# A tuned state-space and gated-MLP kernel: the first table load ahead of two weight loads, tile 1's gate steps split around later transposes, a gated load queue, two warm-up matmuls fewer

## The chip, the cores and the metric

The kernel runs on one core of one Trainium2 chip. Its time is the device time of one execution in microseconds (us); the figure for a kernel is the median of several runs. A core has five engines that run side by side: TensorE (PE, matmuls; PEld is its weight loads), VectorE (DVE), ScalarE (ACT), GpSimd (POOL) and SyncE (SP, here a queue that only issues transfers). Each takes its instructions in the order in which they were written for it, and waits on semaphores for the others.

## The reference

The input x is 2048 tokens of 448 features, in bf16. It is normalised, and two branches use the result: a diagonal complex state-space recurrence (A) and a gated MLP (B).

```python
xn = _layernorm(x, axis=-1)
s = _A_ref(xn, A_Lambda_re, ..., A_Dskip)
g = _silu(_B_ref(xn, B_w_gate, B_w_up, B_w_down))
return x + s * g

# A: per state p, over 2048 steps
Lam_bar = exp(dt * Lam)
Bu = einsum("bld,pd->blp", x, ((Lam_bar - 1) / Lam)[:, None] * Bmat)
h = Lam_bar * h + Bu[:, t]
y = 2 * einsum("blp,dp->bld", hseq, Cmat).real + x * Dskip
# B: 448 -> 1792 -> 448
h = sigmoid(x @ w_gate) * (x @ w_up)
return h @ w_down
```

## The kernel before

The tokens go in four chunks of 512, a chunk being four tiles of 128 tokens. For each chunk TensorE computes 14 gate and up steps of 128 columns (`gu_mm`, L767 and L768: two matmuls at a time, on the two halves of the array's rows), the input products of the recurrence (L841 to L858), the down projection (L983) and the output of the recurrence (L1012). ScalarE evacuates the gates (L801), VectorE the up products (L804) and does the recurrence as a scan (L922).

Only the head differs between the kernels: the time until the first chunk's normalised x stands transposed in SBUF. Tiles 0 to 3 of chunk 0 go through it one by one:

- `load_x` brings tile t; tiles 0 and 2 are issued on SP's queue, 1 and 3 on ScalarE's. `load_w0` brings the first two 128-column blocks of the gate weights (m = 0 and 1) in four parts: A and B for each half of the partitions; the rest of the gate weights (`load_w("SP", "g", ...)`), x for chunk 1, and the up weights follow on SP's queue.
- VectorE takes mean and variance (`bn` L448, `aggr` L454), ScalarE the square root (`root` L482, which needs the square-root table, L412), VectorE the reciprocal (`recip` L479) and the normalised tile (`norm` L515). GpSimd appends a copy of the first 64 columns (L524).
- TensorE transposes the tile against the identity (`pe_transpose` L552, and L554 for the piece that needs GpSimd's copy) into two banks: pieces 4 to 6 make half "b", pieces 0 to 3 half "a". Each half is copied to SBUF by ScalarE (L562) or VectorE (L564), as `split` says.
- `last_tile` (L784 and L785) runs the gate steps m = 0 and 1 for one tile alone, its half "b" or "a". For tiles 0, 1 and 3 this helper is used, for tile 2 `gu_mm` (L767 and L768, 128 columns wide). Step m = 2 is the first over all 512 tokens.
- `columns` (L596, L598) turns three small parameter rows into columns, in the bank `acc[0]` that tile 0's half b has left; ScalarE copies them out (L603), and GpSimd computes the rotation angles from them (`turns`, L614 on). `silu_table` loads ScalarE's second table (L626).
- Before all that, TensorE runs warm-up matmuls on zeros (`warm_mm`, L442).

The order of the work on each engine is made at build time. `Plan.add` takes each operation with an estimated cost, `Plan.solve` computes due times from the order of TensorE's operations and then lists the others by them. TensorE's order is the order of the calls. While `pl.seq` is set (the head), VectorE's and ScalarE's orders are the order of the calls too; operations with `chain=True` keep their order on their engine. `slot` counts the transfers: the ninth waits for the first, and so on.

Of the kernel before, what the change touches and what calls it, by code (L numbers as in the profile page):

```python
# [14 lines left out]
ACT = mybir.ActivationFunctionType  # L15
# [11 lines left out]
TPC = L // P  # L27
# [219 lines left out]
def kernel(  # L247
# [118 lines left out]
    def load_w(eng, k, half, b, r=(), rate=105e3, land=0.0):  # L366
        m0, m1 = BLK[k][b]
        ps = slice(half * H, half * H + H)
        c0 = half * 896
        load(eng, [("w", k, half, m) for m in range(m0, m1)], H * 7 * (m1 - m0) * P * 2,  # L370
             wgt[k][ps, :, m0 * P:m1 * P],
             wsrc[k][:, c0 + m0 * P:c0 + m1 * P].rearrange("(s p) f -> p s f", p=H), cost=0.65, r=r, rate=rate, land=land)

    def load_w0(eng, half, part, land=0.0):
        ps = slice(half * H, half * H + H)
        s0, c0 = (1 - half if part == "A" else half), half * 896
        n = 4 - s0
        load(eng, [("w", "g", half, m, part) for m in range(2)], H * n * 2 * P * 2, wgt["g"][ps, s0:7:2, 0:2 * P],
             wsrc["g"][:, c0:c0 + 2 * P].rearrange("(s p) f -> p s f", p=H)[:, s0:7:2, :], cost=0.5, rate=400e3, land=land)
# [22 lines left out]
    def load_p(eng, k, r=()):  # L402
# [2 lines left out]
    load_x(1, 1, "ACT")  # L405
    load_x(2, 1, "SP", rate=180e3)
    load_x(3, 1, "ACT", rate=180e3)
    load_w0("SP", 0, "A", land=6.5)
    load_w0("ACT", 1, "A", land=6.7)
    load_w0("SP", 0, "B", land=7.2)  # L410
    load_w0("ACT", 1, "B", land=7.5)
    add("ACT", 0.05, lambda: A.preload_act_table_set("sqrt_and_others"), w=["sqrttab"], lat=1.3, chain=True)  # L412
    load_w("SP", "g", 0, 1, rate=400e3, land=8.8)
    load_w("SP", "g", 1, 1, rate=400e3, land=9.8)
    load_w("SP", "g", 0, 2, rate=400e3, land=11.2)
    load_w("SP", "g", 1, 2, rate=400e3, land=12.6)
    load_x(4, 2, land=14.0)
    load_p("POOL", 0)
    load_p("POOL", 1)
    load_p("POOL", 2)  # L420
    add("POOL", 0.15, lambda: G.memset(ident[:], 0.0), w=["ident"], chain=True)
    add("POOL", 0.4, lambda: G.affine_select(out=ident[:], in_=ident[:], compare_op=ALU.not_equal, fill=1.0, base=0,
                                             pattern=[[-1, P]], channel_multiplier=1), r=["ident"], w=["ident"], chain=True)
    add("POOL", 0.1, lambda: G.memset(halfc[:], 0.5), w=["consts"])
    add("POOL", 0.1, lambda: G.memset(negc[:], -1.0), r=["consts"], w=["consts"])
    add("POOL", 0.1, lambda: G.memset(expc[:], math.e), w=["expc"])
# [18 lines left out]

    def bn(t):
        b = t % 3
        add("DVE", 0.6, lambda: V.bn_stats(out=bst[b][:], in_=x_all[:, t, :]),  # L448
            r=[("x", t)] + ([("xnT", 0, 3, "a")] if 3 < t < 8 else []), w=[("bst", b)])

    def aggr(t):
        b = t % 3
        o = (mvf if t < TPC else mv)[:, t, :]
        add("DVE", 0.16, lambda: V.bn_aggr(out=o, in_=bst[b][:]), r=[("bst", b)], w=[("mv", t)])  # L454

    def stats(t):
        bn(t)
# [18 lines left out]

    def recip(t0, n):
        ks = lambda k: [(k, t) for t in range(t0, t0 + n)]
        add("DVE", 0.13, lambda: V.reciprocal(out=rsd[:, t0:t0 + n, :], in_=sdb[:, t0:t0 + n, :]), r=ks("sd"), w=ks("rs"))  # L479

    def root(t):
        add("ACT", 0.3, lambda: A.activation(sdb[:, t, :], mvf[:, t, 1:2], ACT.Sqrt, bias=epsc[:]),  # L482
            r=[("mv", t), "sqrttab", "epsc"], w=[("sd", t)])

    def chain(t0, n):
        ts = range(t0, t0 + n)
# [25 lines left out]
    def norm(t):  # L512
        b, o = xkey(t), xbuf(t)
        if t < TPC:
            add("DVE", 0.42, lambda: V.tensor_scalar(out=o[:, 0:448], in0=x_all[:, t, :],  # L515
                                                     scalar1=mvf[:, t, 0:1], scalar2=rsd[:, t, :],
                                                     op0=ALU.subtract, op1=ALU.mult),
                r=[("x", t), ("mv", t), ("rs", t)], w=[("xn", b)])
        else:
            add("ACT", 0.65, lambda: A.activation(o[:, 0:448], x_all[:, t, :], ACT.Identity,  # L520
                                                 bias=nmr[:, t, :], scale=rsd[:, t, :]),
                r=[("x", t), ("rs", t), ("nm", t)], w=[("xn", b)])
        n = H if t < TPC else D
        add("POOL", 0.25 if n == H else 0.6, lambda: G.tensor_copy(out=o[:, D:D + n], in_=o[:, 0:n]),  # L524
            r=[("xn", b)], w=[("xnw", b)])
# [16 lines left out]
    def pe_transpose(t, parts, between=None):  # L542
        b, js, o = xkey(t), slice(t * P, t * P + P), xbuf(t)
        tp = {}
        for lo, hi, key, bank, eng in parts:
            for s in range(lo, hi):
                tp[s] = flat(bank.bitcast(BF16)[:, 0:(hi - lo) * P], hi - lo, P)[:, s - lo, :]

        def f():
            for s in (4, 5, 6, 0, 1, 2):  # L550
                c0 = s * P if s < 4 else H + (s - 4) * P
                T.transpose(tp[s], o[:, c0:c0 + P], ident[:, :])  # L552
        add("PE", 0.34, f, r=[("xn", b), "ident"], w=[p[2] for p in parts])
        add("PE", 0.06, lambda: T.transpose(tp[3], o[:, 384:512], ident[:, :]), r=[("xnw", b)], w=[parts[-1][2]])  # L554
        for i, (lo, hi, key, bank, eng) in enumerate(parts):
            if i and between:
                between()
            n = (hi - lo) * P
            w = [("xnT", 0, t, h) for h in (("a" if lo == 0 else "b") if len(parts) == 2 else "ab")]
            src = flat(bank.bitcast(BF16)[:, 0:n], hi - lo, P)  # L560
            if eng == "ACT":
                add("ACT", 0.05 + n / 1120.0, lambda src=src, lo=lo, hi=hi: A.copy(out=xnT[0][:, lo:hi, js], in_=src), r=[key], w=w)  # L562
            else:
                add("DVE", 0.07 + n / 1600.0, lambda src=src, lo=lo, hi=hi: V.tensor_copy(out=xnT[0][:, lo:hi, js], in_=src), r=[key], w=w)  # L564
# [60 lines left out]
    def silu_table():  # L625
        add("ACT", 1.3, lambda: A.preload_act_table_set("silu_and_others"), r=[("sd", t) for t in range(4)] + [("xnT", 0, 2, "a")], w=["silutab"])  # L626

    def tables():
        turn = C("turn")
        for pt in range(4):  # L630
            vk, nk = ("v", pt), ("nu", pt)
            v, nu = v_t[:, pt, :], nu_t[:, pt, :]
            add("ACT", 0.61, lambda v=v, pt=pt: A.activation(v, iota[:, 0:NTAB], ACT.Copy, scale=turn[:, pt:pt + 1]),
                r=[("wv", 0), "turn", "silutab"], w=[vk])
            add("DVE", 0.4, lambda v=v, nu=nu: V.tensor_single_scalar(out=nu, in_=v, scalar=MAGIC, op=ALU.add),
                r=[vk], w=[nk])
            add("DVE", 0.6, lambda v=v, nu=nu: V.scalar_tensor_tensor(out=nu, in0=nu, scalar=-MAGIC, in1=v,
                                                                      op0=ALU.add, op1=ALU.subtract),
                r=[vk, nk], w=[nk])
            add("ACT", 0.5, lambda v=v, nu=nu: A.activation(v, nu, ACT.Abs), r=[nk, "silutab"], w=[vk])  # L640
            so, co = (spm[:, pt, 0, :], cosT[:, pt, :]) if pt < 3 else (cs3[:, 1, :], cs3[:, 0, :])
            add("ACT", 0.537, lambda so=so, nu=nu: A.activation(so, nu[:, 0:L], ACT.Sin, scale=-S),
                r=[nk, "silutab"], w=[("sin", pt)])
            add("ACT", 0.624, lambda co=co, v=v: A.activation(co, v[:, 0:L], ACT.Sin, scale=-S, bias=pio2[:]),
                r=[vk, "silutab", "pio2"], w=[("cos", pt)])
            if pt < 3:
                add("DVE", 0.2, lambda pt=pt: V.tensor_single_scalar(out=spm[:, pt, 1, :], in_=spm[:, pt, 0, :],
                                                                     scalar=-1.0, op=ALU.mult),
                    r=[("sin", pt)], w=[("nsin", pt)])
# [390 lines left out]


    warm_mm(9)
    warm_mm(2, 128)
    pl.seq = True
    slots0 = [next_gu() for _ in range(3)]
    u2 = slots0[2]
# [16 lines left out]
    bn(3)  # L1063
    root(2)
    aggr(3)
    split(1, uk, ub, ("ACT", "ACT"), lambda: root(3))
    recip(2, 1)
    norm(2)
    last_tile(0, "g", steps01, 0, "b")
    pv_copy = columns(acc[0][:], ("acc", 0))  # L1070
    pv_copy()
    last_tile(0, "g", steps01, 0, "a")
    recip(3, 1)
    norm(3)
    last_tile(0, "g", steps01, 1)
    add("NONE", 0.0, lambda: None, r=["pv0", ("xnw", 3)], w=["pv"], lat=0.0)
    turns()
    split(2, ak, ab, ("ACT", "DVE"))
    split(3, uk, ub, ("DVE", "DVE"))
    gate(uk, ("gu", u2))  # L1080
    silu_table()
    pl.seq = False
    for m in range(2):
        gu_mm(0, "g", m, slots0[m], 2, 3, m == 0)
    last_tile(0, "g", steps01, 3)
# [112 lines left out]
```

## Time and profile before

| | |
|---|---|
| median of 3 runs | 185.27 us (185.1 to 185.68) |
| the profiled execution | 184.37 us |
| its span (first to last instruction) | 182.6 us |
| PE busy | 177.6 us, 97% |
| DVE / ACT / POOL busy | 165.8 / 96.9 / 39.7 us |
| chain that ended last | PE 93%, DVE 3% |
| gate step m = 2 starts | 11.40 us |
| up step m = 0 starts | 18.95 us |

Times in the views are microseconds from the start of the span. In a timeline a row gives the start, the time taken, the engine, the line of the kernel, the operation, what it writes and reads, and how many instructions were merged; in brackets stands how long the engine had been idle and what ended that. A "q" behind an engine's name (SPq, ACTq) is its queue issuing transfers. The chain of waits goes back from the last instruction and gives at each step what released it. Matmuls are pipelined: a record lasts longer than the distance to the next one, so rates are read from starts.

### The profile page before, as it was taken

To read this page: it belongs to the slowest core of one execution; us is meant where nothing else is said; L and a number is where in the kernel's file an instruction comes from. 1 tells how busy PE (TensorE), PEld (TensorE's weight loads), DVE (VectorE), ACT (ScalarE), POOL (GpSimd) and SP (SyncE) were. 2 spreads that over 40 slices of the span, in tenths; PEclk is the share of its full clock that TensorE was granted. 3 is DMA by queue.
4 is the path that set the end of the run, shared out by engine and by line. 5 is a ranking of instruction groups with operands and counts; after the bars stand their busy time and mean duration, and the time that the engine had idled before them with its cause. 6 is when DMAs were issued, how large, how long until landed. Compare 5 with 4: busy or idle time off the path is not lost.

```text
span 182.6 us, 3617 instructions
## 1 busy us (share of the span) xinstructions
PE 177.6 (97%) x1412; PEld 89.9 (49%) x1412; DVE 165.8 (91%) x295; ACT 96.9 (53%) x158; POOL 39.7 (22%) x95
## 2 busy tenths in 40 slices
PE   7999999999999999999999999999999999999992
PEld 2775555564554444445554444444555444455551
DVE  3759799899989899999999999999999999999763
ACT  3699997959698796364145543348110533411100
POOL 6383458000049956400004100000000000000000
PEclk9999999999999999999999999999999999999999
DMA  5999999998000290000004900002000000002120
GB/s 150 239 222 219 204 163 165 342 153 242 6 0 0 51 154 0 4 0 0 0 2 82 148 0 0 4 0 70 9 0 0 25 27 29 0 5 71 56 77 25
DMA packets 29938, 13.43 MB, mean 74 GB/s; under 512 B 19424, under 2 KB 29920, under 8 KB 29920
## 3 DMA queue, kind: packets, MB, share of 16 engines
q1 hardware_dynamic: 29056, 12.74, 33.9%
q10 hardware_dynamic: 768, 0.46, 0.9%
q8 instruction: 11, 0.18, 0.4%
q14 instruction: 7, 0.06, 0.1%
q0 software_dynamic: 96, 0.00, 0.0%
HBM read 6.77 MB, written 1.84 MB: 47 GB/s over the span
## 4 chain that ended last, share of the span: by engine, by line
PE 93%; DVE 3%; POOL 1%; issue 1%; ACT 1%; DVEq 0%; POOLq 0%
PE gu L767 43%; PE gu L983 15%; PE acc L1012 11%; PE acc L983 9%; PE gu L855 9%; PE acc L858 2%; PE gu L841 2%; PE gu L768 2%; POOL hF L357 1%; PE acc L767 1%; DVE bst L448 1%; PE gu L784 1%; DVE g_t L515 0%; ACT sdb L482 0%; DVE o_t L1028 0%
## 5 line engine op out<-in xcount | busy, mean ns | idle before, releaser
L767 PE MATMUL gu<-xnT,wU 64*128 64x512 bf16 x196 | 45.8, 376 | 0.0
L768 PE MATMUL gu<-xnT,wU 64*128 64x512 bf16 x196 | 45.8, 376 | 0.0
L767 PE MATMUL gu<-xnT,wG 64*128 64x512 bf16 (+2 forms) x203 | 42.3, 350 | 0.1
L768 PE MATMUL gu<-xnT,wG 64*128 64x512 bf16 (+2 forms) x203 | 42.3, 350 | 0.0
L801 ACT ACTIVATE sig<-gu 128x1024 f32<-128x1024 f32 x21 | 21.3, 1020 | 23.7 <-PE gu L768 19.1
L983 PEld LDWEIGHTS <-hF 128*128 128x128 bf16 x224 | 21.9, 98 | 20.6
L767 PEld LDWEIGHTS <-wU 64*128 64x128 bf16 x196 | 18.4, 94 | 22.1
L767 PEld LDWEIGHTS <-wG 64*128 64x128 bf16 x210 | 19.2, 94 | 19.4
L983 PE MATMUL gu<-wd,hF 128*128 128x448 bf16 x140 | 28.0, 352 | 0.0
L804 DVE SCALAR_TENSOR_TENSOR hF<-sig,gu 128x1024 bf16<-128x1024 f32 x21 | 25.4, 1210 | 1.2 <-ACT sig L801 1.0
L922 DVE TENSOR_TENSOR_SCAN wv<-c_r,st,z 128x512 bf16<-128x512 f32 x18 | 22.9, 1277 | 0.0
L1012 PE MATMUL acc<-cT,hT 128*128 128x448 bf16 (+1 forms) x112 | 22.6, 346 | 0.0
L989 ACT ACTIVATE g_t<-gu 128x448 bf16<-128x448 f32 x10 | 5.4, 542 | 27.7 <-PE gu L983 16.8
L768 PEld LDWEIGHTS <-wG 64*128 64x128 bf16 x210 | 19.2, 94 | 0.1
L768 PEld LDWEIGHTS <-wU 64*128 64x128 bf16 x196 | 18.4, 94 | 0.0
L983 PE MATMUL acc<-wd,hF 128*128 128x448 bf16 x84 | 16.9, 352 | 0.0
L855 PE MATMUL gu<-xnT,bT 128*128 128x512 bf16 x72 | 16.7, 379 | 0.0
L1012 PEld LDWEIGHTS <-hT 128*128 128x128 bf16 x119 | 11.5, 98 | 10.1 <-issue 0.4
L869 ACT CAST bus<-gu 128x1024 bf16<-128x1024 f32 x12 | 12.0, 1011 | 6.0 <-PE gu L841 5.5
L524 POOL COPY xn<-xn 128x448 bf16<-128x448 bf16 x12 | 8.2, 698 | 26.2 <-ACT xn L520 26.0
L1024 DVE TENSOR_TENSOR o_t<-acc,xd 128x448 bf16<-128x448 f32 (+1 forms) x16 | 9.6, 601 | 2.7 <-PE acc L1012 2.6
L875 ACT CAST bus<-acc 64x256 bf16<-64x256 f32 (+1 forms) x24 | 8.7, 369 | 5.6 <-PE acc L858 5.3
(149 smaller groups left out, 260.0 us busy)
## 6 DMA issues: line engine op xcount, KB each, us to landing
out_dram<-o_t SPq DMA_DIRECT2D x15, 112.0 KB, 1.7
wd<-in_B_w_down_dram SPq DMA_DIRECT2D x2, 784.0 KB, 6.9
wU<-in_B_w_up_dram SPq DMA_DIRECT2D x2, 448.0 KB, 11.6
x_all<-in_A_x_dram SPq DMA_DIRECT2D x2, 448.0 KB, 4.6
wG<-in_B_w_gate_dram SPq DMA_DIRECT2D x2, 336.0 KB, 6.3
wU<-in_B_w_up_dram SPq DMA_DIRECT2D x2, 336.0 KB, 9.0
wG<-in_B_w_gate_dram SPq DMA_DIRECT2D x2, 224.0 KB, 4.7
x_all<-in_A_x_dram SPq DMA_DIRECT2D x2, 224.0 KB, 8.9
```

The source lines that it names most:

```text
L524: add("POOL", 0.25 if n == H else 0.6, lambda: G.tensor_copy(out=o[:, D:D + n], in_=o[:, 0:n]), r=[("xn", b)], w=[("xnw", b)])
L767: T.matmul(bank[0][:, ts], lhsT=w_[0:H, s, ms], rhs=x[0:H, SL[s], ts], start=(s == 0), stop=(s == 6))
L768: T.matmul(bank[1][:, ts], lhsT=w_[H:P, (s + 1) % 7, ms], rhs=x[H:P, SL[s], ts], start=(s == 0), stop=(s == 6))
L801: add("ACT", act(1024), lambda: A.activation(th, gu[a][:], ACT.Tanh, scale=0.5), r=[("gu", a)], w=[tk])
L804: add("DVE", dve1(1024), lambda: V.scalar_tensor_tensor(out=ho, in0=th, scalar=1.0, in1=gu[a][:], op0=ALU.add, op1=ALU.mult), r=[("gu", a) ...
L855: T.matmul(gu[slots[pt]][:, i, :], lhsT=bT[:, kt, i, pt * P:pt * P + P], rhs=x[:, kt, :], start=(first and kt == 0), stop=(not first and k ...
L869: add("ACT", act(1024), lambda: A.copy(out=bus[u][:], in_=gu[slots[pt]][:]), r=key(pt), w=[("bus", u)])
L875: add("ACT", 0.36, lambda ns=ns, d=d, q=q, l=l, i=i: A.copy(out=bus[u][d, l, ns], in_=acc[a3[i]][q, 0:256]), r=[("acc", a3[i])] + ([("bus" ...
L922: dve(1.194, lambda k=k: V.tensor_tensor_scan(out=wv[:, k, :], data0=rb, data1=z[:, k, :], initial=(st[pt][:, k, :] if c else 0.0), op0=AL ...
L983: T.matmul(d, lhsT=hF[c % 2][:, m, h, js], rhs=wd[:, ft, :], start=(ft == 0), stop=(ft == FT - 1))
L1012: T.matmul(y, lhsT=hT[c % 2][:, hm, js], rhs=cT[:, cm, c0:c1], start=(i == 0 and not on_pe), stop=(i == 6))
L1024: add("DVE", dve1(n), lambda od=od, y=y, c0=c0, c1=c1: V.tensor_tensor(out=od, in0=y, in1=xq[:, c0:c1], op=ALU.add), r=[key, ("xd", q)], w ...
```

## The change

The square-root table load is written before ScalarE's two weight loads, not behind them. The remaining gate weights are written behind the identity and a small GpSimd memset into the region that the first of these loads fills, so that this load waits for the memset. Inside tile 1's evacuation, tile 0's half b steps, the columns and their copy come before the third root; of tile 1's gate steps, half b stays and half a goes behind the transposes of tiles 2 and 3. The first `Copy` of the tables (L633) is issued in the head's fixed order. The two 128-column warm-up matmuls are gone. Several estimates of costs and landing times for the planner are altered (only some are shown).

```diff
     load_x(3, 1, "ACT", rate=180e3)
-    load_w0("SP", 0, "A", land=6.5)
-    load_w0("ACT", 1, "A", land=6.7)
-    load_w0("SP", 0, "B", land=7.2)
-    load_w0("ACT", 1, "B", land=7.5)
     add("ACT", 0.05, lambda: A.preload_act_table_set("sqrt_and_others"), w=["sqrttab"], lat=1.3, chain=True)
-    load_w("SP", "g", 0, 1, rate=400e3, land=8.8)
-    load_w("SP", "g", 1, 1, rate=400e3, land=9.8)
-    load_w("SP", "g", 0, 2, rate=400e3, land=11.2)
-    load_w("SP", "g", 1, 2, rate=400e3, land=12.6)
-    load_x(4, 2, land=14.0)
+    load_w0("SP", 0, "A", land=5.7)
+    load_w0("ACT", 1, "A", land=5.9)
+    load_w0("SP", 0, "B", land=6.9)
+    load_w0("ACT", 1, "B", land=6.9)
     load_p("POOL", 0)
     load_p("POOL", 1)
     load_p("POOL", 2)
     add("POOL", 0.15, lambda: G.memset(ident[:], 0.0), w=["ident"], chain=True)
     add("POOL", 0.4, lambda: G.affine_select(out=ident[:], ...
+    add("POOL", 0.1, lambda: G.memset(wgt["g"][0:1, 0, 256:258], 0.0), w=[("w", "g", 0, m) for m in (2, 3)], chain=True)
+    load_w("SP", "g", 0, 1, rate=400e3, land=8.8)
+    load_w("SP", "g", 1, 1, rate=400e3, land=9.8)
+    load_w("SP", "g", 0, 2, rate=400e3, land=11.2)
+    load_w("SP", "g", 1, 2, rate=400e3, land=12.6)
+    load_x(4, 2, land=14.0)
...
-        add("PE", 0.34, f, r=[("xn", b), "ident"], w=[p[2] for p in parts])
+        add("PE", 0.64 if t < 2 else 0.34, f, r=[("xn", b), "ident"], w=[p[2] for p in parts])
...
+    def scale(pt):
+        turn, v = C("turn"), v_t[:, pt, :]
+        add("ACT", 0.61, lambda: A.activation(v, iota[:, 0:NTAB], ACT.Copy, scale=turn[:, pt:pt + 1]),
+            r=[("wv", 0), "turn", "silutab"], w=[("v", pt)])
+
     def tables():
...
-            add("ACT", 0.61, lambda v=v, pt=pt: A.activation(v, iota[:, 0:NTAB], ACT.Copy, scale=turn[:, pt:pt + 1]),
-                r=[("wv", 0), "turn", "silutab"], w=[vk])
+            if pt:
+                scale(pt)
...
     warm_mm(9)
-    warm_mm(2, 128)
...
     root(2)
     aggr(3)
-    split(1, uk, ub, ("ACT", "ACT"), lambda: root(3))
+
+    def pv_root():
+        last_tile(0, "g", steps01, 0, "b")
+        columns(acc[0][:], ("acc", 0))()
+        root(3)
+    split(1, uk, ub, ("ACT", "ACT"), pv_root)
     recip(2, 1)
     norm(2)
-    last_tile(0, "g", steps01, 0, "b")
-    pv_copy = columns(acc[0][:], ("acc", 0))
-    pv_copy()
     last_tile(0, "g", steps01, 0, "a")
+    last_tile(0, "g", steps01, 1, "b")
     recip(3, 1)
     norm(3)
-    last_tile(0, "g", steps01, 1)
     add("NONE", 0.0, lambda: None, r=["pv0", ("xnw", 3)], w=["pv"], lat=0.0)
     turns()
     split(2, ak, ab, ("ACT", "DVE"))
     split(3, uk, ub, ("DVE", "DVE"))
     gate(uk, ("gu", u2))
     silu_table()
+    scale(0)
     pl.seq = False
+    last_tile(0, "g", steps01, 1, "a")
     for m in range(2):
         gu_mm(0, "g", m, slots0[m], 2, 3, m == 0)
     last_tile(0, "g", steps01, 3)
```

More of the change, by code (lines that the diff above doesn't have):

```diff
@@ L447, in bn @@
         b = t % 3
-        add("DVE", 0.6, lambda: V.bn_stats(out=bst[b][:], in_=x_all[:, t, :]),
+        add("DVE", 0.56 if t < TPC else 0.6, lambda: V.bn_stats(out=bst[b][:], in_=x_all[:, t, :]),
             r=[("x", t)] + ([("xnT", 0, 3, "a")] if 3 < t < 8 else []), w=[("bst", b)])
@@ L453, in aggr @@
         o = (mvf if t < TPC else mv)[:, t, :]
-        add("DVE", 0.16, lambda: V.bn_aggr(out=o, in_=bst[b][:]), r=[("bst", b)], w=[("mv", t)])
+        add("DVE", 0.1 if t < TPC else 0.16, lambda: V.bn_aggr(out=o, in_=bst[b][:]), r=[("bst", b)], w=[("mv", t)])
     def stats(t):
@@ L478, in recip @@
         ks = lambda k: [(k, t) for t in range(t0, t0 + n)]
-        add("DVE", 0.13, lambda: V.reciprocal(out=rsd[:, t0:t0 + n, :], in_=sdb[:, t0:t0 + n, :]), r=ks("sd"), w=ks("rs"))
+        add("DVE", 0.08, lambda: V.reciprocal(out=rsd[:, t0:t0 + n, :], in_=sdb[:, t0:t0 + n, :]), r=ks("sd"), w=ks("rs"))
     def root(t):
-        add("ACT", 0.3, lambda: A.activation(sdb[:, t, :], mvf[:, t, 1:2], ACT.Sqrt, bias=epsc[:]),
-            r=[("mv", t), "sqrttab", "epsc"], w=[("sd", t)])
+        add("ACT", 0.2, lambda: A.activation(sdb[:, t, :], mvf[:, t, 1:2], ACT.Sqrt, bias=epsc[:]),
+            r=[("mv", t), "sqrttab", "epsc"], w=[("sd", t)], lat=0.16)
     def chain(t0, n):
@@ L514, in norm @@
         if t < TPC:
-            add("DVE", 0.42, lambda: V.tensor_scalar(out=o[:, 0:448], in0=x_all[:, t, :],
+            add("DVE", 0.33, lambda: V.tensor_scalar(out=o[:, 0:448], in0=x_all[:, t, :],
                                                      scalar1=mvf[:, t, 0:1], scalar2=rsd[:, t, :],
@@ L552, in f @@
                 T.transpose(tp[s], o[:, c0:c0 + P], ident[:, :])
-        add("PE", 0.34, f, r=[("xn", b), "ident"], w=[p[2] for p in parts])
-        add("PE", 0.06, lambda: T.transpose(tp[3], o[:, 384:512], ident[:, :]), r=[("xnw", b)], w=[parts[-1][2]])
+        add("PE", 0.64 if t < 2 else 0.34, f, r=[("xn", b), "ident"], w=[p[2] for p in parts])
+        add("PE", 0.1 if t < 2 else 0.06, lambda: T.transpose(tp[3], o[:, 384:512], ident[:, :]), r=[("xnw", b)], w=[parts[-1][2]])
         for i, (lo, hi, key, bank, eng) in enumerate(parts):
@@ L626, in silu_table @@
         add("ACT", 1.3, lambda: A.preload_act_table_set("silu_and_others"), r=[("sd", t) for t in range(4)] + [("xnT", 0, 2, "a")], w=["silutab"])
+    def scale(pt):
+        turn, v = C("turn"), v_t[:, pt, :]
+        add("ACT", 0.61, lambda: A.activation(v, iota[:, 0:NTAB], ACT.Copy, scale=turn[:, pt:pt + 1]),
+            r=[("wv", 0), "turn", "silutab"], w=[("v", pt)])
     def tables():
-        turn = C("turn")
         for pt in range(4):
```

## The prediction

> **What bounds the kernel now.** I read the page's busy shares and its chain first, then a table of stretches, then the chain of waits in the first ten microseconds, then each engine's timeline there.
>
> From the page, the busy shares:
>
> ```profile
> PE 177.6 (97%) x1412; PEld 89.9 (49%) x1412; DVE 165.8 (91%) x295; ACT 96.9 (53%) x158; POOL 39.7 (22%) x95
> ```
>
> From the table of stretches (stretch, its length, busy time of PE, PEld, DVE, ACT and POOL with instruction counts, then granted clock, DMA share, GB/s):
>
> ```profile
> 7.93:8.20 0.27, 0.16 (x6) 0.04 (x1) 0.27 (x1) 0.27 (x2) 0.20 (x1) 1.00 0.97 252
> ...
> 9.72:9.84 0.12, 0.00 (x1) 0.01 (x2) 0.08 (x2) 0.12 (x1) 0.12 (x1) 1.00 1.07 265
> ...
> 11.40:178.00 166.60, 166.60 (x1256) 82.56 (x1250) 158.10 (x270) 90.26 (x146) 33.15 (x68) 1.00 0.33 66
> ```
>
> From 11.40 us, where the gate step m=2 starts, to 178.00 TensorE has no idle time. So the end is that start plus a constant, and whatever the head gains or loses is found again at the end, as long as no wait appears later. TensorE is idle in the head: before 8.20 its only records are the tails of pipelined matmuls, and before 9.84 it does nothing. The chain of waits says who ends these gaps:
>
> ```profile
> 4.35 0.29 ACT sdb L482
> 4.64 0.02 issue
> 4.66 0.16 DVE rsd L479
> 4.83 0.08 DVE mvf L454
> 4.91 0.35 DVE g_t L515
> ...
> 5.87 0.55 DVE bst L448
> ...
> 6.62 0.52 DVE bst L448
> ...
> 7.38 0.30 ACT sdb L482
> 7.68 0.48 ACT xnT L562
> ...
> 8.82 0.44 PE acc L552 x6
> ...
> 9.36 0.44 DVE xnT L564
> ```
>
> Three things last: the first root (L482) starts late and holds VectorE's chain of statistics; ScalarE's second copy of tile 1 (7.58 to 8.15) holds tile 1's second half of gate steps at 8.20, and behind these in TensorE's order stand the transposes of tiles 2 and 3, whose input was ready at 7.83 (tile 2, L515); VectorE's copy of tile 2 (9.36 to 9.78) holds the steps of 9.84. Why the root is late, from ScalarE's timeline:
>
> ```profile
> 1.66 1.34 ACTq L357 DMA_DIRECT2D wG<-in_B_w_gate_dram  x2
> 3.04 1.28 ACT L412 ACT_TABLE_LOAD   x1 [3.04 <-issue]
> 4.33 0.30 ACT L482 ACTIVATE sdb<-mvf,epsc 128x1 bf16<-128x1 f32 x1
> ```
>
> The root starts where the table load ends (3.04 + 1.28 = 4.32). Its variance was ready at 3.96 (L454, 3.78 + 0.18). The chain names a GpSimd memset as its releaser, but that ends at 4.34, after the root's start, and the memset of epsc that the root reads ends at 3.67.
>
> **Part 1: the table load before the two weight loads on ScalarE's queue.** It would start at 1.66 and end at 2.94, under the wait for x. The root is then bound by its variance: 3.96 + 0.04 (the gap from L454 to the second root: 4.74 + 0.16 to 4.94) = 4.00 instead of 4.33. VectorE gets less of it, since it is in bn_stats of tile 1 until 3.88 + 0.59 = 4.47; that tile's aggregate then starts at 4.51 instead of 4.74. All later VectorE steps move by that 0.23: norms at 4.63, 5.24, 7.20 and 7.70, tile 0's transposes at 5.08, tile 1's at 5.69, tile 0's first gate steps at 6.19 (6.42 before). They read the weight halves A, landed by 1.66 + 4.1 = 5.76. No row shows whether a transfer is issued while a table load runs. Bounds: the issues go out at 1.66 as now (cost nothing), or at 2.94 (1.28 later). I take the first: the profile books issues to ACTq and table loads to ACT. In the second case the root is again behind the two issues (2.94 + 1.34 = 4.28), the 0.23 is lost and the first gate steps wait for a later half A.
>
> [...]
>
> **Part 2: tile 1's gate steps split.** Order on TensorE now: tile 0 (halves b, columns, a), tile 1 (b, a), transposes 2, transposes 3, steps of tile 2. After: tile 1's b, transposes 2 and 3, tile 1's a, steps of tile 2. Nothing is added; the two waits get cover:
> - Tile 1's a follows transposes 3, at about 8.7. Its copy now ends at 8.15; it moves 0.23 earlier with the roots and 0.18 later behind the copy of the columns (L603, 0.18), so it ends near 8.1. The 0.27 of idle before 8.20 goes.
> - Transposes of tile 2 start at about 7.8 (their norm ends at 7.60), not 8.75. VectorE's copy of tile 2 then runs 8.41 to 8.83, under tile 1's a (8 slots of 56 ns, 0.45, until 9.14). The gap of 9.49 to 9.84 falls from 0.35 between starts to the 0.15 seen at the same change of work at 6.27 to 6.42: 0.20 goes.
> - Tile 3's copies (0.69 for both) end near 9.5, before its steps at 9.9.
>
> **Part 3: columns' copy ahead of the third root.** The root of tile 3 needs its aggregate at 7.12 and the copy ends at 7.24, so that root is some 0.1 later than it could be; tile 3's norm (7.70) is needed only by 8.2. Free. GpSimd's chain starts after tile 3's pad copy in both.
>
> **Part 4: SP's loads of blocks 1 and 2 behind a GpSimd memset.** The memset stands after the identity, at about 3.57, and lasts 0.10 like its neighbours; epsc moves 0.04, with 0.3 to spare. The first load now issues at 3.31 and would at 3.72: +0.41, with everything queued behind it on SP (the rest of wG, x 4 to 7, wU, dbc, the transposes of B). Landings now are 7.8 and 8.8 (issue 3.31 + 4.5, 4.02 + 4.8), against the need at 10.75; the second half of wU's first block lands at 7.34 + 10.1 = 17.44, against a need at 18.95 - 0.65 = 18.3. Even the whole 0.41 leaves 0.45. It need not arrive, as the transfers' share is full from 2 us on and x and the first weights are still landing until 6.9. For the same reason I book no gain for the first weight halves. Half B, issued at 2.42, lands at 6.92 (+ 4.5), and this now matters: tile 0's second half would be ready to run at 6.90. Bounds: 0.3 later (a share of the ring lost to something else) to 0.2 earlier; I take 6.92, start 6.95.
>
> **Part 5: two 128-column warm-up matmuls gone** (4.99 to 5.3). TensorE waits for the norm there anyway, so the time itself is free; what they do for TensorE's pace is the first rival. The first scaling of the position table (L633) joins the written order where it already ran, behind the second table load (10.93), and the changed cost figures alter only the planner's order, for which the last rival stands.
>
> **The sum.** From tile 0's second half to step m=2: now 7.13 to 11.40 = 4.27, less 0.27 and 0.20 of idle = 3.80. After: 6.95 + 3.80 = 10.75, that is 0.65 earlier. The profiled execution took 184.37 (span 182.6 and 1.77 around it): 183.72. The median of the runs is 0.90 above it; taking the same 0.65 off 185.27 gives **184.62**. Later covers hold: VectorE waits 1.22 us for TensorE at 172.32, and the last state write for chunk 3 ends at 167.6, against its first use at 170.8.
>
> **The rivals.**
> *Slower: TensorE's slow pace lasts longer.* The page prints a granted clock of 1.00 throughout, but the warm-up matmuls start 0.427 apart (loads of weights at 1.58, 2.01, 2.44) where the same 512 columns later take 0.215 (11.40, 11.61, 11.83). The pace rises while tile 0 is transposed: its six take 0.59, tile 1's 0.51.
>
> ```profile
> 5.31 0.59 PE L552 MATMUL acc<-ident,g_t 128*128 128x128 bf16 x6
> ...
> 5.92 0.51 PE L552 MATMUL gu<-ident,g_t 128*128 128x128 bf16 x6
> ```
>
> After the change the warm-up ends near 5.0 and its end is what keeps TensorE busy until then. At half pace each slot of 128 columns costs 0.055 more. Tiles 1 to 3's transposes and the steps between are 41 slots: 2.26 at worst, 186.9. The point of decision is 12 slots (0.65 / 0.055) for no gain, 22 for a loss that can be measured; I price it at 30, 1.65 - 0.65 = +1.0, **186.3**. Against it: TensorE's gap before the transposes stays at 0.1 (now 5.10 + 0.11 to 5.31; after, 4.57 + 0.43 to 5.08), so it is no less busy than now.
>
> [...]
>
> *Partial.* The same slow pace over tiles 0 and 1 only (up to the copies' own pace): 7 slots are 0.39 off the gain, or half B lands 0.3 later: gain 0.25 to 0.5, **184.9**.
>
> *The table load blocks ScalarE's queue* (the change doesn't do what it says): the 0.23 is gone and half A lands up to 0.5 later; part 2 remains: gain about 0.2, **185.05**.
>
> *A later wait.* Earlier due times reorder VectorE or ScalarE behind TensorE. Nothing in the trace shows one; from -0.1 to a copy's length, +1.2: **185.6**.
>
> **How the numbers follow.** Forecast 0.54 (own range 184.4 to 184.8), partial 0.20, blocked queue 0.06, slow pace 0.14, later wait 0.06. 0.3% is 0.56 us, about what a measurement of this kernel can tell from no change. Faster by more: nearly all of the forecast, 0.52. Slower by more: the slow pace and part of the later wait, 0.18. Within: 0.30. The range runs from 184.2 (half B early, and the runs' own scatter of 0.2) to 186.0, leaving out the upper part of the slow pace.
>
> **What would show it.** Right: table load at 1.7, first root at 4.0, tile 2's transposes at 7.8, no TensorE gap after 7.0, step m=2 at 10.7 to 10.8. Wrong: weight issues on ACTq after 2.9; transposes of tile 1 taking 0.7; m=2 later than 11.1; any TensorE gap after it.

## The result, and the profile after

The changed kernel took **184.24 us** (median of 12 runs, 184.01 to 185.0) against 185.05 for the kernel before in the runs beside it (12 runs, 184.45 to 185.68): ratio 0.996, 95% interval 0.9943 to 0.9976, that is 0.4 to 1.05 us less. Two later series gave 0.9958 (0.9941 to 0.9975) and 0.9956 (0.9936 to 0.9975). The forecast was 184.62, a gain of 0.65; measured were 0.81, 0.68 and 0.78. The comparison moved from 185.27 to 185.05 with more runs, which is 0.22 of the 0.38 by which the time lies below the forecast.

The profiled execution of the changed kernel, though, took 184.25 us with a span of 182.4, only 0.12 below the profiled one before, and not 0.65. From its page, the busy shares:

```profile
PE 177.7 (97%) x1410; PEld 88.8 (49%) x1410; DVE 166.3 (91%) x295; ACT 97.0 (53%) x158; POOL 38.1 (21%) x96
```

They say nothing of the change but the two matmuls fewer. The table of stretches, from a little before tile 0's first gate steps to step m=2, and from there to 178.00 (columns as in the prediction):

```profile
6.50:11.26 4.76, 4.76 (x134) 4.22 (x134) 2.81 (x9) 3.44 (x9) 2.53 (x9) 1.00 1.04 229
11.26:178.00 166.74, 166.74 (x1256) 81.47 (x1251) 158.60 (x270) 90.84 (x146) 31.92 (x70) 1.00 0.34 67
```

Both gaps of before (0.27 and 0.20) are gone and no new one has appeared; yet m=2 starts at 11.26, not 10.75. ScalarE's timeline (rows as in the prediction) shows the first half of the change at work:

```profile
1.66 1.28 ACT L408 ACT_TABLE_LOAD   x1 [1.66 <-PEq L1190]
1.69 1.60 ACTq L357 DMA_DIRECT2D wG<-in_B_w_gate_dram  x2
4.15 0.30 ACT L483 ACTIVATE sdb<-mvf,epsc 128x1 bf16<-128x1 f32 x1 [1.21 <-DVE mvf L455]
```

The table load starts at 1.66, and the two weight issues run beside it from 1.69: the load does not hold the queue. The root waits for its variance now (L455), at 4.15. So 0.18 of the hoped 0.33 came. The rest of the lateness is in TensorE's timeline, the transposes of tiles 0 and 1:

```profile
5.13 0.82 PE L553 MATMUL acc<-ident,g_t 128*128 128x128 bf16 x6
5.75 0.31 PE L555 MATMUL acc<-ident,g_t 128*128 128x128 bf16 x1
5.85 0.85 PE L553 MATMUL gu<-ident,g_t 128*128 128x128 bf16 x6
6.49 0.31 PE L555 MATMUL gu<-ident,g_t 128*128 128x128 bf16 x1
```

Six transposes take 0.82 and 0.85, against 0.59 and 0.51 before. From the first of six to the seventh it is 5.75 - 5.13 = 0.62, or 0.103 each; at full pace, for tile 2 of the same profile, it is 8.70 - 8.35 = 0.35, or 0.058 each. In the table of stretches TensorE is "busy" all this time and its granted clock is printed as 1.00:

```profile
4.00:6.00 2.00, 2.00 (x12) 1.02 (x11) 1.89 (x8) 0.93 (x3) 0.81 (x5) 1.00 0.86 234
```

So neither column shows the half pace; starts do. The chain of waits agrees: from the warm-up matmuls on it never leaves TensorE.

```profile
3.49 1.71 PE gu L443 x4
5.20 0.75 PE acc L553 x6
5.95 0.11 PE acc L555
6.06 0.64 PE gu L553 x6
6.70 0.11 PE gu L555
```

The same kernel profiled again (run `e5_after`: 183.64 us, span 181.9) has full pace from tile 0 on:

```profile
4.99 0.51 PE L553 MATMUL acc<-ident,g_t 128*128 128x128 bf16 x6 [0.34 <-DVE g_t L516]
5.34 0.22 PE L555 MATMUL acc<-ident,g_t 128*128 128x128 bf16 x1
5.66 0.51 PE L553 MATMUL gu<-ident,g_t 128*128 128x128 bf16 x6
```

There the root is at 4.01, tile 2's transposes at 7.76 and m=2 at 10.67: the forecast's timeline (4.00, 7.8, 10.75) and its time for the profiled execution (183.72).

### The profile page after: what moved, and what is told of

Same layout as the page of the kernel before. It is cut to its first block, busy times and chain, and to the rows that moved or that the text cites. A ratio compares the mean times of both kernels' runs of the same rounds, so it can differ in the third digit from the quotient of the medians.

```text
span 182.4 us, 3618 instructions
## 1 busy us (share of the span) xinstructions
PE 177.7 (97%) x1410; PEld 88.8 (49%) x1410; DVE 166.3 (91%) x295; ACT 97.0 (53%) x158; POOL 38.1 (21%) x96
## 4 chain that ended last, share of the span: by engine, by line
PE 97%; DVE 1%; issue 0%; DVEq 0%
PE gu L772 44%; PE gu L988 15%; PE acc L1017 11%; PE acc L988 9%; PE gu L860 9%; PE gu L443 2%; PE acc L863 2%; PE gu L846 2%; PE gu L789 1%; PE acc L772 1%; PE gu L773 1%; PE acc L553 1%; PE gu L553 1%; DVE o_t L1033 0%; PE acc L849 0%; DVE o_t L1029 0%
## 5 line engine op out<-in xcount | busy, mean ns | idle before, releaser
L449 DVE BATCH_NORM_STATS2 bst<-x_all 128x6 f32<-128x448 bf16 x12 | 7.0, 611 | 6.7 <-DMA x_all<-in_A_x_dram 6.7
```

The lines of the kernel that those rows point to most:

```text
L449: add("DVE", 0.56 if t < TPC else 0.6, lambda: V.bn_stats(out=bst[b][:], in_=x_all[:, t, :]), r=[("x", t)] + ([("xnT", 0, 3, "a")] if 3 < ...
```

## The experiments

Each row is read from a run's TensorE timeline and from its series. "Half a" is the start of tile 0's second half of gate steps, "x0" the start of tile 0's bn_stats, "six" the time of the six transposes of tiles 0 and 1. The comparison is with the kernel before in the same series: its own median moved between 184.41 and 185.05 from one series to the next, so medians of different series can be compared only loosely.

| run | x0 | root | six | half a | m=2 | difference | median; before beside it | ratio, 95% |
|---|---|---|---|---|---|---|---|---|
| before | 3.12 | 4.33 | 0.59, 0.51 | 7.14 | 11.40 | 4.26 | | |
| after | 3.21 | 4.15 | 0.82, 0.85 | 7.46 | 11.26 | 3.80 | 184.24; 185.05 | 0.996 (0.9943 to 0.9976) |
| e1_nogate | 3.12 | 4.06 | 0.82, 0.60 | 7.47 | 12.19 | 4.72 | 185.14; 184.41 | 1.0037 (1.0012 to 1.0063) |
| e2_warm11 | 3.29 | 4.24 | 0.51, 0.51 | 7.10 | 10.89 | 3.79 | 184.22; 184.41 | 0.9995 (0.9972 to 1.0017) |
| e3_table | 3.25 | 4.20 | 0.51, 0.51 | 7.06 | 11.76 | 4.70 | 185.07; 184.41 | 1.0027 (1.0016 to 1.0039) |
| e4_split | 3.26 | 4.34 | 0.51, 0.51 | 7.14 | 10.94 | 3.80 | 183.95; 184.41 | 0.9969 (0.9958 to 0.998) |
| e5_after | 3.07 | 4.01 | 0.51, 0.51 | 6.87 | 10.67 | 3.80 | 184.06; 184.74 | 0.9958 (0.9941 to 0.9975) |
| e6_split_gate | 3.27 | 4.33 | 0.82, 0.64 | 7.38 | 11.18 | 3.80 | 184.11; 184.74 | 0.9966 (0.9952 to 0.998) |
| e7_split_table_1b | 3.30 | 4.24 | 0.51, 0.51 | 7.10 | 10.90 | 3.80 | 183.94; 184.74 | 0.9955 (0.9938 to 0.9972) |
| e8_warm4 | 3.22 | 4.33 | 0.82, 0.85 | 7.98 | 12.07 | 4.09 | 185.75; 184.74 | 1.005 (1.0033 to 1.0066) |
| e9_after | 3.19 | 4.13 | 0.82, 0.82 | 7.36 | 11.15 | 3.79 | 184.19; 184.97 | 0.9956 (0.9936 to 0.9975) |
| e10_split | 3.22 | 4.34 | 0.51, 0.51 | 7.14 | 10.94 | 3.80 | 184.19; 184.97 | 0.9958 (0.9941 to 0.9975) |
| e11_split_table_1b | 3.25 | 4.19 | 0.85, 0.80 | 7.46 | 11.26 | 3.80 | 184.24; 184.97 | 0.9953 (0.9937 to 0.9968) |
| e12_table_gate | 3.24 | 4.18 | 0.52, 0.51 | 7.04 | 11.30 | 4.26 | 185.01; 184.97 | 1.0004 (0.9982 to 1.0027) |

**The order alone (e4_split, e10_split).** The kernel before with the new `pv_root` inside tile 1's evacuation and tile 1's half a behind the transposes of tiles 2 and 3; nothing else.

```diff
-    split(1, uk, ub, ("ACT", "ACT"), lambda: root(3))
+    split(1, uk, ub, ("ACT", "ACT"), pv_root)
...
+    last_tile(0, "g", steps01, 1, "b")
...
-    last_tile(0, "g", steps01, 1)
...
+    last_tile(0, "g", steps01, 1, "a")
```

> The kernel before with only the new order: tile 0's b steps, columns and their copy ahead of the third root, and tile 1's half a behind the transposes of tiles 2 and 3. My theory: the two waits of TensorE (0.27 before 8.20, 0.20 before 9.84) go, step m=2 at 10.9 to 11.0, 0.4 to 0.5 us faster than before. Rival (only the parts together help, as each wait is replaced by VectorE's chain): 0 to 0.2 us faster.

> Only the new order of the gate steps, again, side by side with the changed kernel. Theory (the order carries the gain, table load and gate nearly cancel): within 0.25 us of the changed kernel, runs within 0.3 us of each other. Rival (the table load's 0.23 is kept on top, as in the prediction): 0.2 to 0.3 us slower than the changed kernel.

TensorE's timeline around the two waits, first before, then e4:

```profile
7.88 0.22 PE L785 MATMUL gu<-xnT,wG 64*128 64x128 bf16 x1
8.20 0.21 PE L784 MATMUL gu<-xnT,wG 64*128 64x128 bf16 x1
...
9.49 0.22 PE L554 MATMUL gu<-ident,g_t 128*128 128x128 bf16 x1
9.84 0.21 PE L767 MATMUL gu<-xnT,wG 64*128 64x128 bf16 x1
```

```profile
7.88 0.22 PE L785 MATMUL gu<-xnT,wG 64*128 64x128 bf16 x1
8.03 0.51 PE L552 MATMUL acc<-ident,g_t 128*128 128x128 bf16 x6
...
8.77 0.22 PE L554 MATMUL gu<-ident,g_t 128*128 128x128 bf16 x1
8.92 0.23 PE L784 MATMUL gu<-xnT,wG 64*128 64x128 bf16 x1
```

Between starts 0.32 and 0.35 have become 0.15 each. Half a starts at 7.14 as before, and m=2 comes 3.80 later instead of 4.26: 0.46 gained, in the profile as in this series' medians (183.95 against 184.41). In the last series, beside the changed kernel, both have a median of 184.19. The order carries the gain. It does so without the planner's altered estimates and the fixed place of the first `Copy`, which were not run alone.

**The table load alone (e3_table).** The kernel before with the table load written ahead of the weight loads.

```diff
+    add("ACT", 0.05, lambda: A.preload_act_table_set("sqrt_and_others"), w=["sqrttab"], lat=1.3, chain=True)
     load_w0("SP", 0, "A", land=6.5)
...
     load_w0("ACT", 1, "B", land=7.5)
-    add("ACT", 0.05, lambda: A.preload_act_table_set("sqrt_and_others"), w=["sqrttab"], lat=1.3, chain=True)
```

> The kernel before with only the table load moved ahead of ScalarE's two weight loads. My theory: first root at 4.0 to 4.1 us, VectorE's chain and everything behind it 0.23 us earlier, step m=2 at 11.2, about 0.2 us faster than before. Rival (the steps behind are held by something else, so the earlier root is hidden): no change within 0.1 us, m=2 at 11.4.

It is slower than before (1.0016 to 1.0039), although its root is earlier. From its timelines, ScalarE's queue and one row of TensorE:

```profile
1.69 2.33 ACTq L357 DMA_DIRECT2D wG<-in_B_w_gate_dram  x2
```

```profile
7.79 0.23 PE L785 MATMUL gu<-xnT,wG 64*128 64x128 bf16 x1 [0.51 <-DMA wG<-in_B_w_gate_dram]
```

The two issues on ScalarE's queue take 2.33 together, where they took 1.34. The second goes out at 3.42 by its record, not at 2.38, because it has become the ninth transfer: by their records the transfers of the two queues share eight semaphores (in the profile before, the first eight issues, 0.73 to 2.42, have eight different ones; the ninth, at 3.31, has that of tile 1's x, landed at 3.27, and waits on it). In e3 SP's first load of the remaining weights has the eighth, and this half B reuses that of tile 1's x and waits until x has landed (3.40). Half B lands at 7.75 instead of 6.61, and TensorE, ready at 7.06, waits for weights. That the numbering follows the 1.3 us which the build assumes for the table load is my reading; the trace shows only who holds which semaphore.

**The gate taken out (e1_nogate).** The changed kernel without the memset, the remaining gate weights written directly behind the first ones.

```diff
+    load_w("SP", "g", 0, 1, rate=400e3, land=8.8)
...
-    add("POOL", 0.1, lambda: G.memset(wgt["g"][0:1, 0, 256:258], 0.0), w=[("w", "g", 0, m) for m in (2, 3)], chain=True)
-    load_w("SP", "g", 0, 1, rate=400e3, land=8.8)
...
```

> The changed kernel with the remaining gate weights written again right behind the first ones, without the GpSimd memset that delays them. My theory (only the order of TensorE's work and the earlier root matter): the same as the changed kernel within 0.15 us, so about 0.8 us faster than before; first of these loads issued near 3.3 us, last up weights landed near 21.8 instead of 22.99. Rival (the gate shields the first weight halves): half B of SP lands near 6.9 instead of 6.32, and the gain shrinks by 0.1 to 0.3. Other rival (the gate makes the up weights late, landed 22.99 against a need at 23.35): faster than the changed kernel by 0.1 to 0.2.

1.0037: with table load and new order but no gate the kernel is slower than before. The mechanism is that of e3: ScalarE's half B issues at 3.29 and lands at 8.35, and from half a to m=2 it takes 4.72. In this profile ScalarE's half A is late too (6.71), and the first gate steps wait for it from 6.35 to 6.76.

**Table load and gate, old order (e12_table_gate).** The kernel before with the change's whole load section.

```diff
+    add("ACT", 0.05, lambda: A.preload_act_table_set("sqrt_and_others"), w=["sqrttab"], lat=1.3, chain=True)
     load_w0(...)
...
+    add("POOL", 0.1, lambda: G.memset(wgt["g"][0:1, 0, 256:258], 0.0), w=[("w", "g", 0, m) for m in (2, 3)], chain=True)
+    load_w("SP", "g", 0, 1, rate=400e3, land=8.8)
...
```

> The kernel before with the table load ahead of the weight loads AND the GpSimd gate ahead of the remaining gate weights, order of the gate steps as before, warm-ups as before. Theory (the gate is there for the early table load: it keeps ScalarE's second weight load from being put behind a ninth transfer): ScalarE's second weight load issues at 2.4 again, not 3.3 as in the run with the table load alone; the first root is at 4.0 to 4.2, step m=2 at 11.1 to 11.4, time 0.0 to 0.3 us below the kernel before, not 0.5 above. Rival (the early table load costs for another reason, in ScalarE's own order): weight load at 2.4 all the same, but m=2 at 11.7 or later and 0.3 to 0.5 us above the kernel before.

```profile
1.70 1.61 ACTq L357 DMA_DIRECT2D wG<-in_B_w_gate_dram  x2
```

The queue is free again (half B issued at 2.45, landed at 6.54) and m=2 is at 11.30, 0.10 earlier than before. So the gate undoes what the early table load breaks, and the rival that blamed ScalarE's order is out. But the series shows no gain (0.9982 to 1.0027). In the profiled execution the 0.10 is lost again, and more, at a wait near 30.5 us, in the chain of waits:

```profile
29.39 1.14 DVE hF L805
30.53 0.04 issue
30.57 0.39 PE gu L842 x2
```

TensorE stands idle for 0.48 there, until VectorE's product of the gates is done. From the first input product of the recurrence to the next gate step it takes 6.34 in this profile, against 5.52 before.

**The order with the gate, without the early table load (e6_split_gate).**

> The new order alone, plus the GpSimd memset that holds back the remaining gate weights; the table load stays behind ScalarE's weight loads. Theory (the gate is a cost: a dip in the transfers near 6 to 8 us, the stream about 0.4 us later): 0.0 to 0.3 us slower than the order alone, with a few executions held at the up weights. Rival (the gate speeds the first weight halves): up to 0.1 us faster than the order alone.

0.9966 against 0.9958 for the changed kernel beside it: the intervals overlap widely. The gate costs nothing that these runs can tell. What it does to the transfers is seen at the issue: the first remaining block goes out at 3.66 to 3.69 in all six profiles with the gate, at 3.31 before. It then lands at 8.51 here and at 9.01, 8.62 and 8.43 in the changed kernel's three profiles, against 7.85 before; but e10, which has no gate, received it at 9.11, so the landing doesn't tell the two apart. Between 6 and 8 us the transfers' share (last column but one) is lower, first before, then after:

```profile
6.00:8.00 2.00, 2.00 (x52) 1.73 (x53) 1.86 (x8) 1.93 (x6) 0.28 (x2) 1.00 1.09 232
```

```profile
6.00:8.00 2.00, 2.00 (x45) 1.67 (x45) 1.63 (x7) 1.75 (x7) 0.28 (x2) 1.00 0.88 205
```

It is 0.88 to 0.96 in the six profiles with the gate and 0.98 to 1.19 in the eight without. The bandwidth does not follow it: 246 in e5 with the gate, 201 in e10 without.

**Another way to the early table load (e7_split_table_1b, e11_split_table_1b).** The new order, the table load behind ScalarE's first weight load, the second one on SP's queue, no gate.

```diff
     load_w0("ACT", 1, "A", land=6.7)
-    load_w0("SP", 0, "B", land=7.2)
-    load_w0("ACT", 1, "B", land=7.5)
     add("ACT", 0.05, lambda: A.preload_act_table_set("sqrt_and_others"), w=["sqrttab"], lat=1.3, chain=True)
+    load_w0("SP", 0, "B", land=7.2)
+    load_w0("SP", 1, "B", land=7.5)
```

> The new order alone, plus the table load right behind ScalarE's first weight load, and its second one moved to SP's queue, so that no later load takes its transfer slot; no gate. Theory (displaced slot, not the table load, is what costs): no displaced load, first root at 4.0 to 4.15 us, 0.05 to 0.2 us faster than the order alone, that is about 0.55 us faster than before. Rival (issuing a third weight load on SP makes it land late, near 7.3): 0.1 to 0.3 us slower than the order alone.

> New order, table load right behind ScalarE's first weight load, its second one moved to SP's queue, no gate. Theory: 0.0 to 0.25 us below the run with the order alone, by how early x arrives, and at or below the changed kernel, with a small spread. Rival (the fourth load on SP's queue delays the remaining gate weights enough to matter): as the order alone or up to 0.2 us slower.

Its medians are 183.94 and 184.24; e4 and e10 had 183.95 and 184.19, the changed kernel 184.06 and 184.19 beside e7 and e11. I had hoped that it would beat both kernels; in these series it equals the changed one, and in the last series the order alone.

**The warm-up matmuls (e2_warm11, e8_warm4).** e2 is the changed kernel with the two short matmuls back; e8 is the new order with four warm-up matmuls in all.

```diff
     warm_mm(9)
+    warm_mm(2, 128)
```

```diff
-    warm_mm(9)
-    warm_mm(2, 128)
+    warm_mm(4)
...
```

> The changed kernel with the two 128-column warm-up matmuls put back. My theory: they lie in TensorE's wait for the first norm and change nothing: within 0.15 us of the changed kernel. Rival (without them TensorE's pace rises later): 0.3 us faster than the changed kernel, and tile 1's six transposes take 0.5 us, not 0.7.

> The new order alone with 4 warm-up matmuls of 512 columns in place of 9 and the 2 short ones, so that TensorE is idle from 2.9 us to the first transposes at 5.3. Theory (TensorE's pace rises only after some 3 us of work, at a moment that differs between executions): in most executions the pace rises after 7 us, 0.5 to 1.8 us slower than the order alone, with a scatter above 0.5 us. Rival (the warm-up does nothing, the pace rises by itself): within 0.1 us.

e2's median is 184.22. The changed kernel was not run in this series; in others it had 184.06 to 184.24. e2's ratio, 0.9995, is worse than the changed kernel's (0.996), but it stands on a low 184.41 for the kernel before, and three of its twelve runs took 184.96 to 186.36. The profiled one (185.67) shows where such time can go, a row of TensorE's timeline:

```profile
24.07 0.39 PE L773 MATMUL gu<-xnT,wU 64*128 64x512 bf16 x1 [0.53 <-DMA wU<-in_B_w_up_dram]
```

The last block of the up weights landed at 24.03 there (21.73 before) and TensorE waited for it. So the medians leave open what the two short matmuls are worth.

What they do to the pace is told by the starts. In five of the nine profiles that have them (e2, e3, e4, e7, e10) the first of the two lasts 0.22, where it lasts 0.31 at half pace: the pace was full before they began, so they did not bring it. In the other four the pace was still half, and tile 0's six transposes took 0.52 (e12), 0.59 (before), 0.82 (e6) and 0.85 (e11). Without the two they took 0.51 (e5) and three times 0.82 (after, e9, e1). e2's transposes at full pace are what its rival expected, but e2 is one of the five. The last of the long matmuls together with the two short ones, at full pace in e2, then at half pace before:

```profile
4.56 0.70 PE L443 MATMUL gu<-hF 128*128 128x512 bf16 x3
```

```profile
4.57 0.85 PE L442 MATMUL gu<-hF 128*128 128x512 bf16 x3
```

No effect of the two is shown, and with so few profiles none is excluded.

Four warm-up matmuls are too few: 185.75, 1.0033 to 1.0066, with tile 0 reached after a pause of 2.25 and at half pace. Like gate steps start 0.11 apart up to 8.60 and 0.055 apart from 8.67 on, so the rise came 3.3 behind tile 0's first transpose; in e4 the first short step between weight loads, 3.72 to 4.02, ends 2.8 behind the first matmul (1.18). The expectation's "some 3 us" agrees with both.

```profile
5.32 0.82 PE L552 MATMUL acc<-ident,g_t 128*128 128x128 bf16 x6 [2.25 <-DVE g_t L515]
```

**The changed kernel again (e5_after, e9_after).**

> The changed kernel once more, beside the others of this call. Theory (the new order brings 0.45 us, the table load with its gate brings little and makes the weight stream later): about as fast as the order alone or up to 0.3 us slower, that is 0.2 to 0.45 us faster than before, with single executions held up by late up weights. Rival (the parts of the prediction add up): 0.6 to 0.8 us faster than before and 0.2 faster than the order alone.

> The changed kernel once more, as the measure for the next two on the same chip. Expected 0.7 us below the kernel before (0.4 to 0.9), its runs spread over 0.8 us or more.

The gain repeats (0.68 and 0.78), and the runs spread over 1.15 and 1.37 us. The two profiles differ as the pace does: half a at 6.87 and 7.36, m=2 at 10.67 and 11.15.

## Why the prediction was right, point by point

The gain came where the larger part of the sum put it, from the split order. The smaller part, the earlier root, is seen in the profiles at full pace, but no median shows it beyond the noise, and the step from the profiled execution to the median did not hold; that the total agrees so well is in part luck.

- **The end is m=2 plus a constant: right for the changed kernel, not in every execution.** After's m=2 is 0.14 earlier than before's and its profiled time 0.12 less (184.25 against 184.37); e5's 0.73 earlier and 0.73 less; e4's 0.46 and 0.39. But e2 and e12 have the waits at 24 and 30.5 us, and e10, whose m=2 is also 0.46 earlier, was profiled at 184.36, only 0.01 less: the stretch from the first input product of the recurrence to the next gate step (L841 on) took 5.81 there (29.20 to 35.01), 5.52 before (29.53 to 35.05) and 5.86 in e3. "A later wait" was given 0.06 for the change as a whole; in four of the thirteen other profiles (e2, e3, e10, e12) 0.3 or more is lost behind m=2.
- **Part 2, 0.47 for the split: right.** Half a to m=2 was to go from 4.27 to 3.80. It is 4.26 in the two kernels with the old order and no wait for weights (before, e12) and 3.79 or 3.80 in nine of the eleven profiles with the new order; the other two are e1 (wait for weights) and e8 (four warm-ups). This is where the gain comes from.
- **Part 1, earlier root and VectorE chain, half a at 6.95: mechanism right, size too large.** In all nine profiles with the early table load the root starts 0.94 or 0.95 after x0; with the late one at 4.33 or 4.34, whatever x0 does. The prediction took x0 at 3.12 from its one profile. Over those nine runs x0 stands between 3.07 and 3.30, so the root gains 0.09 to 0.32. Where the transposes run at full pace, half a starts 0.27 (e5), 0.04 (e2, e7) and, in the old order, 0.08 and 0.10 (e3, e12) earlier than 7.14. The step was booked at 0.18, to be added to the 0.47 of the order. The medians don't add up like that: in the last series the order alone gains 0.78 and the whole change 0.78, and table load and gate without the order gain nothing (e12). The blocked-queue case is refuted by the issues at 1.69 beside the table load.
- **Part 4, the gate as a pure delay: wrong.** Its price was read rightly, the first load at 3.69 against the 3.72 reckoned. What it is for was missed: without it the early table load makes half B the ninth transfer (e3, e1). The text followed SP's half B, "I take 6.92"; it landed at 6.32 in the changed kernel, and ScalarE's, now the later one, at 6.57, both outside the bound of 0.2 earlier. Without the gate it is ScalarE's half B that comes late, at 7.75 and 8.35. The section counted the transfers' bandwidth, not the eight semaphores that they share (ScalarE's half B was issued at 3.42 in e3 and 3.29 in e1, at 2.38 before), though the helper `slot` was named. That did not harm the total, because the change contained the cure. The cover for the up weights was checked against the first block alone; the one that fails first is the last (24.03 in e2).
- **Part 3 and Part 5, free: nothing contradicts them.** No wait of TensorE after the third root shows; of the two matmuls no effect on the pace is shown, and none is excluded (e2 above).
- **The last step of the sum, 0.90 from the profiled execution to the median: not borne out.** The prediction gave both kernels the same distance. The changed kernel's three profiled executions, 184.25, 183.64 and 184.20, stand beside medians of 184.24, 184.06 and 184.19, so the distance is -0.01, 0.42 and -0.01. The kernel before had been profiled in one of its fastest executions: 184.37, where the fastest of its four series are 184.45, 184.36, 184.37 and 184.38. That is why a gain of 0.12 between the first two profiles stands beside one of 0.81 between the medians, and why the forecast's 184.62 is near the measured time although that profile missed its timeline. What speaks for the 0.65 itself is e5's timeline and the difference of the fastest executions, 0.44, 0.73 and 0.59 in the three series.
- **The pace: the "partial" rival is what the first profile shows.** It priced the slow pace over tiles 0 and 1 at 0.39. After's half a is 0.32 later than with the order alone at full pace (7.46 against 7.14), 0.59 later than in e5 (6.87), of which 0.14 is x0. So the forecast is the early case, the partial rival the late one, and the kernel has both: 183.64 and 184.25 are two executions of it. Not foreseen is that the comparison hardly minds: the gain in the medians stayed at 0.68 to 0.81. The kernel before has one profile, its rise within tile 0's transposes (0.59), so how much it loses with a late rise stays open.

The moment of the rise differs between executions with the same nine warm-ups: in e5 it has come by 4.06 (weight loads below), in the changed kernel's first profile not before 6.49, the start of tile 1's seventh transpose (6.49 - 5.85 = 0.64 from the first of six, 0.107 each). The medians of the changed kernel are 0.68 to 0.81 less in its three series; in which of their runs the rise was late is not on record.

What stays open: why some executions receive the last up weights a microsecond later. In the profiles with the gate they landed at 22.24 to 24.03, in those without it at 21.66 to 23.40; that is no clean separation, and the spread of e10, which has no gate (183.9 to 184.9), speaks against the gate as the only cause. Also open is what delays VectorE at 30.5 in e12.

## What to carry to other kernels

Split a change of a head into parts and run them alone: here one reordering on TensorE carries the gain, and of two further edits one repairs what the other breaks. Before an instruction is moved ahead of transfers, count the transfers in flight on every queue: here they share eight semaphores, and in e3 the one that became the ninth was issued at 3.42, behind another's landing at 3.40, instead of at 2.38. Read the pace from the starts of like instructions, not from busy shares, and take a landing, and the distance from a profiled execution to the median, from more than one execution before it enters a sum.

## What the runs showed of the hardware

- A table load on ScalarE (1.28 us from 1.66) and the issue of two transfers on its queue (from 1.69) run side by side.
- TensorE's pace can rise within 2.9 us of its first matmul: from e5's timeline of weight loads, the step from 3.72 to 4.06 is already short and the load itself 0.10 instead of 0.15, after a start at 1.18. In other executions with the same warm-ups it is still half at 6.4.

```profile
3.72 0.15 PEld L443 LDWEIGHTS <-hF 128*128 128x128 bf16 x1 [0.28 <-issue]
4.06 0.10 PEld L443 LDWEIGHTS <-hF 128*128 128x128 bf16 x1 [0.19 <-issue]
```

- The landing of the same 112 KB of x, issued at 0.72 or 0.73 in every profile, moved the start of tile 0's statistics between 3.07 and 3.30; these 0.23 alone are a third of the forecast gain.
